# A retention, attention and token-mixing kernel: two-stage weight conversion, a later product of the values, other PSUM banks in the first and last batch, and attention outputs issued ahead of a state product

## The chip, the cores and the metric

The kernel runs on one core of a Trainium2 chip. Its engines work at the same time and wait for each other by semaphores: TensorE (PE in the profile; PEld is its weight load) for matrix products, VectorE (DVE), ScalarE (ACT), GpSimd (POOL), and SyncE (SP), whose queue issues nearly all DMA transfers. Each engine takes its instructions strictly in the order of its queue. The metric is the device time of one execution in microseconds (us); lower is better.

## The reference

```python
def _attn_ref(q, k, v):                      # 8 batches, 8 heads, 576 positions, 64 wide
    scores = scale * np.matmul(q, k.transpose(0, 1, 3, 2))
    gamma = 1.0 - 2.0 ** (-5.0 - np.arange(H, dtype=np.float32))
    Dmat = np.where(rel >= 0, gamma[:, None, None] ** rel[None, :, :], 0.0)
    return np.matmul(scores * Dmat[None], v)
def _moe_ref(x, w_gate, wq, wk, wv, wo):     # 4 experts, each position takes 2
    logits = x @ w_gate                      # the two best, softmax over them: the weights w
    for e in range(E):                       # causal softmax attention of every expert
        q = x @ wq[e]; k = x @ wk[e]; v = x @ wv[e]
        ye = softmax(causal(scale * (q @ k.T))) @ v @ wo[e]
        out += mask[..., None] * w[:, :, kk:kk + 1] * ye
def _moe2_ref(x, w_theta, w_tok_r, w_tok_i, w_ch):
    theta = x @ w_theta
    zr, zi = x * np.cos(theta), x * np.sin(theta)
    y = einsum('ts,bsd->btd', w_tok_r, zr) + einsum('ts,bsd->btd', w_tok_i, zi)
    u = x + y
    return u + np.maximum(u @ w_ch, 0.0)
```

The three run one behind the other: retention gives x, the experts' attention gives the next x, and the token mixing gives the result. Several weights come as float64.

## The kernel before

**First stage (0 to about 485 us).** Retention goes by chunks of 128 positions (five in a batch, the last of 64): `ret_scores` (`w<-kt`), `ret_values` (`w<-sm,vp`, then `w<-kt,S`) and `ret_state` (`pS<-vp,kv`), which adds to a state in the PSUM tile `pS`. After each half chunk ACT copies that state to SBUF (`S<-pS`), and the next `ret_state` may write `pS` only then. `ret_step` interleaves the three for one visit, in five visits a batch, which the table `SLOTS` calls R1 to R5. `loads` brings a chunk's keys and values (`kv`) and has POOL scale the values (`vp<-kv,gam`). The chunk's result is split into a rounded part `xh` (ACT) and a rest `xl` (POOL), from which `proj_qk` and `proj_v` project for the experts.

Between the visits the attention of the batch before runs by units of one expert pair and 128 rows: `at_scores`, `at_trans` (transposes through PSUM, copied to `PT` by DVE and ACT), and `at_out` (`w<-PT,V`), whose results ACT copies to `ob`. Also in this stage 52 blocks of float64 weights are converted: `convert` has five integer operations on DVE (`b`, `ex`), two on ACT (`r`, and `hl`, the rounded part) and three on POOL (`r`, `d`, `hl`), and the result is stored to DRAM.

PE stands in the order of the code in this stage. On the other engines, and on all of them later, a scheduler lays the queues out before the run by its own estimate of when each instruction is ready.

**Second stage (from about 485 us).** Eight batches, each with `mix(b, 0)`, some `token_tile`, `mix(b, 1)`, more `token_tile` and four `channel`. A `mix` sums 54 pairs of products, of 256 and 320 columns (`TS`), into four PSUM banks `acc`; DVE then adds them to `u`, ACT rounds them (`uh`), and DVE or POOL takes the rest (`ul`). `channel` puts its sums into banks called `w`. `z_tile` makes the operands of a mix from the angles `nr`: three operations on DVE, a sine on ACT, a product on DVE, then the split into `zh` and `zl`. `load_o` fetches the attention outputs of a batch and has POOL multiply them by the gate weights (`ol<-ol,og`). `x_put` and `x_get` transpose the next batch's input through DRAM.

Of the kernel before, what the change touches and what calls it, by code (L numbers as in the profile page):

```python
# [10 lines left out]
F32 = mybir.dt.float32  # L11
# [21 lines left out]
TS = [(0, 256), (256, 576)]  # L33
CV = 192
# [26 lines left out]
def tile_kernel(ctx: ExitStack, tc: tile.TileContext, qk, kv, w1, wo, wot, wd, cst, out):  # L61
# [20 lines left out]
    ident = consts.tile([128, 128], F32, name="ident")  # L82
    tri = att.tile([128, 64], F32, name="tri")
# [24 lines left out]
    QKT, KVT, XT, PSS, VP, SM, PX = {}, {}, {}, {}, {}, {}, {}  # L108

    def loads(b, c):  # L110
# [77 lines left out]
    def ret_step(b, c, nx):  # L188
# [234 lines left out]
    def convert(cvt, h, l, src, n):  # L423
# [30 lines left out]

    def cvt_jobs(pl, weights):

        def job(dst, off, o, n):
            t = pl.tile([128, 2, n], F32R, name="hl", bufs=2, padded_shape=[128, 2, CV])
            convert(pl, t[:, 0, :], t[:, 1, :], wd[:, off + o:off + o + n], n)
            flush()  # L460
            PEND.append((dst[:, :, o:o + n], t.bitcast(F32)))

        return [lambda a=(dst, off, x, min(CV, w - x)): job(*a) for dst, off, w in weights for x in range(0, w, CV)] + [flush]

# [412 lines left out]
```

## Time and profile before

| what | value |
|---|---|
| time, three runs | 912.73 us median (907.61 to 915.47) |
| profiled execution | 907.77 us, span 905.8 us, mean granted clock 0.992 |
| PE busy / PEld busy | 863.0 us (95%) / 803.9 us (89%) |
| DVE / ACT / POOL busy | 628.8 us (69%) / 454.9 us (50%) / 218.9 us (24%) |
| chain of waits, share by engine | PE 67%, DVE 10%, DMA 8%, ACT 6%, issue 3%, POOL 2%, SP queue 2% |

The span runs from the first to the last instruction. "Busy" of PE counts each product until its modelled end, so products that follow at once overlap. [...] An idle time is given with the instruction that it ends at and what released that one.

### The profile page before, as it was taken

The numbers are of one execution on the slowest core, as the hardware profiler recorded it, in microseconds if no ns is written. First come the engines' busy times: TensorE is split into PE (matmuls) and PEld (weight loads), VectorE is DVE, ScalarE is ACT, GpSimd is POOL, SyncE is SP. The second block draws the span as 40 slices with busy tenths as digits, with TensorE's granted clock in tenths as the row PEclk, the third lists the DMA queues.
The fourth block names the chain that finished last, engine by engine and source line by source line (L and its number), as shares of the span: only waits on it lengthen the run. The fifth ranks groups of instructions, "written<-read, shape, count | busy, mean of one in ns | idle before, by whom it ended". The sixth has DMA issues, their size and how long they took to land.

```text
span 905.8 us, 25503 instructions
## 1 busy us (share of the span) xinstructions
PE 863.0 (95%) x10062; PEld 803.9 (89%) x10062; DVE 628.8 (69%) x1779; ACT 454.9 (50%) x1198; POOL 218.9 (24%) x268
## 2 busy tenths in 40 slices
PE   6998999899999999998999989999999999999998
PEld 6987888788898888888878889999999999999998
DVE  5376767878787776777769947866578764676732
ACT  2466666666666665665656513443244533434320
POOL 2434152452535434242212102001020110001010
PEclk8999999999999999999999999999999999999999
DMA  7857566676667667656795152333425123251401
GB/s 276 237 143 234 159 203 170 187 223 184 194 182 241 167 180 227 163 148 207 202 317 173 30 143 50 62 90 92 128 50 135 35 72 80 37 125 25 106 23 53
DMA packets 146216, 130.30 MB, mean 144 GB/s; under 512 B 83504, under 2 KB 121648, under 8 KB 146096
## 3 DMA queue, kind: packets, MB, share of 16 engines
q1 hardware_dynamic: 145952, 128.39, 50.1%
q8 instruction: 79, 1.29, 0.6%
q0 software_dynamic: 144, 0.28, 0.2%
q14 instruction: 41, 0.34, 0.1%
HBM read 78.03 MB, written 32.00 MB: 121 GB/s over the span
## 4 chain that ended last, share of the span: by engine, by line
PE 67%; DVE 10%; DMA 8%; ACT 6%; issue 3%; POOL 2%; SPq 2%; DVEq 0%; ACTq 0%; POOLq 0%
PE acc L711 22%; PE w L99 9%; PE w L98 9%; PE w L100 9%; PE w L242 4%; PE w L370 4%; PE w L304 3%; DMA kv<-kv 3%; PE w L351 2%; ACT P L312 2%; PE pS L150 2%; DVE P L307 1%; DMA TK<-td 1%; DMA wst<-w 1%; ACT U L225 1%
## 5 line engine op out<-in xcount | busy, mean ns | idle before, releaser
L711 PE MATMUL acc<-TK,zh 128*128 128x256 f32 (+1 forms) x1024 | 180.7, 299 | 3.4 <-ACT zh L103 1.8
L711 PEld LDWEIGHTS acc<-TK,zh 128*128 128x128 f32 x1024 | 155.7, 191 | 4.0 <-issue 3.7
L312 ACT ACTIVATE P<-P,st 128x128 f32<-128x128 f32 (+4 forms) x160 | 95.6, 598 | 55.9 <-DVE st L307 55.5
L711 PE MATMUL acc<-TK,zl 128*128 128x256 f32 (+1 forms) x512 | 110.9, 298 | 0.0
L727 POOL TENSOR_TENSOR ul<-u,uh 128x576 fp32r<-128x576 f32 x16 | 24.3, 1540 | 336.4 <-ACT uh L726 336.4
L307 DVE CUSTOM_DVE_ANT_0 P<-w,cm 128x128 f32<-128x128 f32 (+4 forms) x160 | 71.8, 477 | 24.4 <-PE w L304 24.1
L711 PEld LDWEIGHTS acc<-TK,zl 128*128 128x128 f32 x512 | 87.0, 191 | 0.0
L103 ACT ACTIVATE zh<-cs 128x512 fp32r<-128x512 f32 x64 | 40.4, 631 | 90.2 <-PE acc L711 68.2
L99 PE MATMUL w<-xl,WH 128*128 128x288 f32 x256 | 75.9, 296 | 4.5 <-POOL xl L183 4.5
L567 ACT ACTIVATE cs<-cs 128x512 f32<-128x512 f32 x72 | 45.2, 631 | 69.1 <-DVE cs L565 55.2
L98 PE MATMUL w<-uh,CH 128*128 128x256 f32 (+1 forms) x256 | 75.5, 297 | 2.4 <-ACT uh L726 2.4
L98 PE MATMUL w<-xh,WH 128*128 128x288 f32 x256 | 76.0, 297 | 0.7 <-ACT PT L356 0.7
L104 DVE TENSOR_TENSOR zl<-cs,zh 128x512 fp32r<-128x512 f32 x64 | 44.0, 690 | 46.4 <-ACT zh L103 45.7
L304 PE MATMUL w<-KK,U 128*64 128x288 f32 (+4 forms) x384 | 76.2, 327 | 0.0
L99 PE MATMUL w<-ul,CH 128*128 128x256 f32 (+1 forms) x256 | 75.7, 296 | 0.0
L100 PE MATMUL w<-uh,CH 128*128 128x256 f32 (+1 forms) x256 | 75.6, 296 | 0.0
L100 PE MATMUL w<-xh,WL 128*128 128x288 f32 x256 | 75.4, 295 | 0.0
L150 PE MATMUL pS<-vp,kv 64*64 64x64 f32 x1024 | 44.0, 226 | 19.8 <-ACT S L153 15.9
L442 POOL TENSOR_TENSOR r<-r,ex 128x192 f32<-128x192 f32 (+1 forms) x51 | 29.5, 579 | 136.4 <-ACT hl L443 61.8
L569 DVE SCALAR_TENSOR_TENSOR cs<-cs,x 128x512 f32<-128x512 f32 x72 | 48.7, 687 | 18.6 <-ACT cs L567 18.4
L304 PEld LDWEIGHTS w<-KK,U 128*128 128x128 f32 (+1 forms) x384 | 53.9, 171 | 7.5 <-issue 4.3
L150 PEld LDWEIGHTS pS<-vp,kv 64*64 64x64 f32 x1024 | 35.8, 137 | 27.1 <-ACT S L153 18.5
(140 smaller groups left out, 2267.2 us busy)
## 6 DMA issues: line engine op xcount, KB each, us to landing
KK<-KN SPq DMA_DIRECT2D x128, 144.0 KB
kt<-qk SPq DMA_DIRECT2D x32, 512.0 KB
kv<-kv SPq DMA_DIRECT2D x32, 512.0 KB
raw<-wd SPq DMA_DIRECT2D x43, 192.0 KB
xd<-xb SPq DMA_DIRECT2D x126, 64.0 KB
out<-u SPq DMA_DIRECT2D x28, 288.0 KB
u<-xd SPq DMA_DIRECT2D x28, 288.0 KB
td<-hl SPq DMA_DIRECT2D x27, 192.0 KB
```

Source lines behind the costliest of these rows:

```text
L98: nc.tensor.matmul(ps, ah, bh, start=first, stop=False)
L99: nc.tensor.matmul(ps, ah, bl, start=False, stop=False)
L100: nc.tensor.matmul(ps, al, bh, start=False, stop=last)
L103: nc.scalar.activation(h, src, AF.Copy)
L104: nc.vector.tensor_sub(l, src, h)
L150: nc.tensor.matmul(pS[half(s), x, :], u[half(s), j, 0, x * D:x * D + D], vp[half(s), j, x, :], start=k == 0 and x == 0, stop=False, skip_g ...
L304: nc.tensor.matmul(ps[s][:R], U[:, s, rs], KK[:, s, x, j0:j1], start=x == 0, stop=x == 1)
L307: MARK["dve"] = nc.vector.tensor_tensor_reduce(Ps[s][:R, j0:j1], ps[s][:R], cm[:R, o + j0:o + j1], 1.0, st[:R, 0, s:s + 1] if i else 3.0e3 ...
L312: MARK["act"] = nc.scalar.activation(Ps[s][:R, :n], Ps[s][:R, :n], AF.Exp, bias=st[:R, last, s:s + 1], scale=-1.0, accum_out=SUM[p][:R, m, ...
L567: nc.scalar.activation(cs, cs, AF.Sin)
L569: nc.vector.scalar_tensor_tensor(z, cs, -1.0, x2[:, None, ds].to_broadcast([128, 2, 256]), op0=OP.mult, op1=OP.mult)
L711: nc.tensor.matmul(acc[d][j], A[:, dc], TK[:, kt, W, t0:t1], start=q == 0 and n == 0, stop=q == 8 and n == 2)
```

## The change

Seven edits:

1. `convert` ends after the first sums and returns `rest` (POOL's product and sums, ACT's `hl`), which the next block's job runs first. Its small tiles have two buffers, and the store goes out one job later.
2. `loads` no longer has the values scaled; `scale` does that at the end of a later visit.
3. `ret_step` takes `mid`, which issues the visit's `at_out`s ahead of the last state product.
4. The gate product of `load_o` waits for the channel products issued last (from batch 1 on).
5. In `z_tile`, DVE's subtraction of half pi becomes a bias of ACT's sine, which is split into two.
6. `mix` (from batch 1 on) and `channel` use equal halves of 288 columns (`TH`).
7. In batches 0 and 7, `mix(b, 1)` sums into the banks `w` and `channel` into the banks `acc`. In batch 0 `x_put` stands among the channels.

```diff
+TH = [(0, 288), (288, 576)]
...
-        vp = ret.tile([128, 2, 4, D], F32, name="vp", bufs=VPB)
-        MARK["pool"] = nc.gpsimd.tensor_mul(vp[:, :n], u[:, :n, 1, :].rearrange("p j (h d) -> p j h d", h=4),
-                                            gam[:, c, :n, :, None].to_broadcast([128, n, 4, D]))
-        QKT[b, c], KVT[b, c], VP[b, c] = t, u, vp
+        QKT[b, c], KVT[b, c] = t, u
+        RAW.append((b, c))
+
+    def scale_v(b, c):
+        n = ROWS[c] // 64
+        vp = VP[b, c] = ret.tile([128, 2, 4, D], F32, name="vp", bufs=VPB)
+        MARK["pool"] = nc.gpsimd.tensor_mul(vp[:, :n], KVT[b, c][:, :n, 1, :].rearrange("p j (h d) -> p j h d", h=4),
+                             gam[:, c, :n, :, None].to_broadcast([128, n, 4, D]))
+
+    def scale():
+        if RAW:
+            scale_v(*RAW.pop(0))
...
-            if nx[1] < NCH - 1:
-                diag.append(ret_state(nx[0], 2 * nx[1]))
         if c >= 0:
             off.append(ret_values(b, c))
-        for _ in zip_longest(chain(*diag), chain(*off)):
+        last = nx and nx[1] < NCH - 1
+        off = chain(*off)
+        for _, _ in zip_longest(chain(*diag), islice(off, 12) if last and mid else off):
             pass
+        if mid:
+            mid()
+        for _ in zip_longest(ret_state(nx[0], 2 * nx[1]) if last else (), off):
+            pass
+        if (b, c) > (0, 1):
+            scale()
...
-        nc.gpsimd.tensor_mul(r, r, ex.bitcast(F32))
-        nc.scalar.activation(h, v, AF.Copy)
-        d = tmp("d", F32)
-        nc.gpsimd.tensor_sub(d, v, h)
-        nc.gpsimd.tensor_add(l, d, r)
...
+        def rest():
+            nc.gpsimd.tensor_mul(r, r, ex.bitcast(F32))
+            nc.scalar.activation(h(), v, AF.Copy)
+            nc.gpsimd.tensor_sub(v, v, h())
+            nc.gpsimd.tensor_add(l(), v, r)
+
+        return rest
...
+    def finish():
+        flush()
+        if REST:
+            rest, pl, n, dst = REST.pop()
+            t = pl.tile([128, 2, n], F32R, name="hl", bufs=2, padded_shape=[128, 2, CV])
+            HL[:] = [t]
+            rest()
+            PEND.append((dst, t.bitcast(F32)))
...
-        nc.gpsimd.tensor_mul(OL[b], OL[b], gw)
+        m = nc.gpsimd.tensor_mul(OL[b], OL[b], gw)
+        if "ch" in MARK:
+            tc.add_manual_dep(m.ins, MARK["ch"].ins.name, mybir.DependencyInfo(
+                mybir.DependencyClass.Sync, mybir.DependencyReason.DATA), reason="behind the channel products")
...
-        nc.vector.tensor_scalar(cs[:, 0, :], cs[:, 0, :], math.pi / 2.0, None, op0=OP.subtract)
         nc.vector.tensor_scalar(cs[:, 1, :], nr[:, ds], PI_LO, -PI_LO, op0=OP.min, op1=OP.max)
-        nc.scalar.activation(cs, cs, AF.Sin)
+        nc.scalar.activation(cs[:, 0, :], cs[:, 0, :], AF.Sin, bias=quarter)
+        nc.scalar.activation(cs[:, 1, :], cs[:, 1, :], AF.Sin)
...
-                ret_step(x, c - 1, (x, c) if c < NCH else (x + 1, 0) if x + 1 < B else None)
-                for o in outs:
-                    at_out(*o)
-                outs = []
+                def mid():
+                    for o in outs:
+                        at_out(*o)
+                    outs.clear()
+
+                ret_step(x, c - 1, (x, c) if c < NCH else (x + 1, 0) if x + 1 < B else None, mid)
...
-        acc = [[ps2.tile([128, t1 - t0], F32, name=f"acc{d}{i}", bufs=1, padded_shape=[128, 512])
-                for i, (t0, t1) in enumerate(TS)] for d in range(2)]
+        ts = TH if b else TS
+        spare = h and b in EDGE
+        acc = [[ps2.tile([128, t1 - t0], F32, name="w" if spare else f"acc{d}{i}", bufs=4 if spare else 1,
+                         padded_shape=[128, 512]) for i, (t0, t1) in enumerate(ts)] for d in range(2)]
...
+    EDGE = (0, B - 1)
...
-        for t0, t1 in TS:
-            ps = ps2.tile([128, t1 - t0], F32, name="w", bufs=4, padded_shape=[128, 512])
+        for j, (t0, t1) in enumerate(TH):
+            spare = b in EDGE
+            ps = ps2.tile([128, t1 - t0], F32, name=f"acc{et % 2}{j}" if spare else "w", bufs=1 if spare else 4,
+                          padded_shape=[128, 512])
...
         for et in range(4):
             channel(b, et)
+            for x in q[2 * et:2 * et + 2] if not b else []:
+                x_put(*x)
+        if not b:
+            x_get(1)
```

The visit R1, on PE. `w<-PT,V` are the attention outputs, `pS<-vp,kv` the visit's last state product, `w<-kt,S` the last products of the values. Before:

```order
L134 MATMUL w<-kt 64x64 x2
L170 MATMUL w<-kt,S_134 64x64 x2
L150 MATMUL pS<-vp,kv 64x64 x8
L370 MATMUL w<-PT,V 64x128 x2
L370 MATMUL w<-PT,V 64x256 x4
L370 MATMUL w<-PT,V 64x128 x2
L304 MATMUL w<-KK,U 64x288 x8
```

And now:

```order
L145 MATMUL w<-kt 64x64 x2
L181 MATMUL w<-kt,S_136 64x64 x2
L387 MATMUL w<-PT,V 64x128 x2
L387 MATMUL w<-PT,V 64x256 x4
L387 MATMUL w<-PT,V 64x128 x2
L161 MATMUL pS<-vp,kv 64x64 x8
L321 MATMUL w<-KK,U 64x288 x8
```

The outputs have moved ahead of the state product; R3 and R5 change in the same way, while R2 has no outputs and R4 no last state product.

The visit R3, on ACT, between the exponentials of a unit and `xh`. `r` and `hl` belong to a conversion. Before:

```order
L312 ACTIVATE P,sum_127<-P,st 128x128 x2
L441 ACTIVATE r<-raw 128x192
L443 ACTIVATE hl<-b_2392 128x192
L245 COPY V<-w 128x256
L246 ACTIVATE lg_124<-w 128x4
L356 COPY PT<-w 128x4x64
L358 COPY PT<-w 64x64
L153 ACTIVATE S_135<-pS 128x256
L153 ACTIVATE S_136<-pS 128x256
```

And now:

```order
L329 ACTIVATE P,sum_129<-P,st 128x128 x2
L465 ACTIVATE hl<-b_2228 128x128
L461 ACTIVATE r<-raw 128x192
L262 COPY V<-w 128x256
L263 ACTIVATE lg_126<-w 128x4
L373 COPY PT<-w 128x4x64
L375 COPY PT<-w 64x64
L164 ACTIVATE S_137<-pS 128x256
L391 COPY ob<-w 128x192
L164 ACTIVATE S_138<-pS 128x256
```

`hl` now belongs to the block before (its size differs from that of `r`), and the copy of an attention output stands between the two state copies.

POOL, two visits of one batch, with the buffers' numbers, which count up in the order of the code (`kv_2069` is loaded at the end of the visit whose result is `xt_2063`). Before:

```order
L119 TENSOR_TENSOR vp_2071<-kv_2069,gam_121 128x512
L183 TENSOR_TENSOR xl_2062<-xt_2063,xh_2061 128x4x128
L442 TENSOR_TENSOR r_2244<-r_2244,ex_2240 128x128
L445 TENSOR_TENSOR d_2248<-b1_2237,hl_2234 128x128
L446 TENSOR_TENSOR hl_2234<-d_2248,r_2244 128x128
L119 TENSOR_TENSOR vp_2232<-kv_2230,gam_121 128x256
L183 TENSOR_TENSOR xl_2062<-xt_2224,xh_2061 128x4x128
```

And now:

```order
L127 TENSOR_TENSOR vp_2218<-kv_2086,gam_123 128x512
L194 TENSOR_TENSOR xl_2079<-xt_2080,xh_2078 128x4x128
L466 TENSOR_TENSOR b1_1960<-b1_1960,hl_2221 128x192
L464 TENSOR_TENSOR r_2235<-r_2235,ex_2231 128x128
L467 TENSOR_TENSOR hl_2221<-b1_1960,r_1967 128x192
L127 TENSOR_TENSOR vp_2372<-kv_2216,gam_123 128x256
L194 TENSOR_TENSOR xl_2079<-xt_2210,xh_2078 128x4x128
```

The product of the values just loaded (`kv_2086` with `xt_2080`) still stands directly ahead of that visit's `xl`; only the operations of the conversions have moved.

POOL, at the end of the first stage. `ol<-ol,og` are gate products, `ul<-u,uh` belongs to the first mixes. Before:

```order
L446 TENSOR_TENSOR hl<-d,r 128x128
L520 TENSOR_TENSOR ol<-ol,og 128x1152 x2
L727 TENSOR_TENSOR ul<-u,uh 128x576 x4
L520 TENSOR_TENSOR ol<-ol,og 128x1152
L727 TENSOR_TENSOR ul<-u,uh 128x576 x2
```

And now:

```order
L467 TENSOR_TENSOR hl<-b_8315,r 128x128
L770 TENSOR_TENSOR ul<-u,uh 128x576 x2
L556 TENSOR_TENSOR ol<-ol,og 128x1152
L770 TENSOR_TENSOR ul<-u,uh 128x576 x2
L556 TENSOR_TENSOR ol<-ol,og 128x1152
L770 TENSOR_TENSOR ul<-u,uh 128x576 x2
```

The two gate products of batches 2 and 3 have left the end of the first stage and stand behind the `ul` of batch 0 and of batch 1.

## Rows read from the trace of the kernel before

**Rows 1.** Windows: us; then busy us (instructions) by engine, granted clock, DMA.
```profile
150.00:200.00 50.00, 46.23 (x842) 41.63 (x840) 40.03 (x130) 32.89 (x103) 22.74 (x31) 1.00 0.69 198
700.00:750.00 50.00, 50.00 (x344) 48.08 (x343) 35.16 (x81) 20.80 (x37) 5.77 (x3) 1.00 0.30 77
```

**Rows 2.** Waits of PE, 50 to 410 us: total us, times, longest.
```profile
PE pS L150 <- ACT S L153: 12.8, 17, 2.1
PE w L99 <- POOL xl L183: 4.5, 5, 1.9
PE w L242 <- POOL xl L183: 1.7, 1, 1.7
```

**Rows 3.** Waits of PE, 410 to 906 us.
```profile
PE w L98 <- ACT uh L726: 2.4, 1, 2.4
PE acc L711 <- ACT zh L103: 1.8, 1, 1.8
PE acc L711 <- DVE u L725: 1.6, 1, 1.6
...
PE acc L711 <- DVE u L723: 1.5, 1, 1.5
```

**Rows 4.** Timeline of PE, a visit R1: start, duration, instructions, idle before.
```profile
164.93 0.23 PE L170 MATMUL w<-kt,S 64*64 64x64 f32 x2
165.72 0.68 PE L150 MATMUL pS<-vp,kv 64*64 64x64 f32 x16 [0.56 <-ACT S L153]
166.33 1.52 PE L370 MATMUL w<-PT,V 128*64 128x128 f32 x16
```

**Rows 5.** Timeline of ACT, the same visit.
```profile
165.11 0.27 ACT L358 COPY PT<-w 128x128 f32<-128x128 f32 x1
165.26 0.40 ACT L153 ACTIVATE S<-pS 128x256 f32<-128x256 f32 x1
```

**Rows 6.** Timeline of all engines, a visit R3.
```profile
176.06 1.43 DVE L434 SCALAR_TENSOR_TENSOR b<-raw,b 128x192 int32<-128x192 int32 x1
...
177.92 0.36 ACT L443 ACTIVATE hl<-b 128x192 fp32r<-128x192 f32 x1 [1.26 <-DVE b L438]
...
178.43 0.20 DVE L358 COPY PT<-w 64x64 f32<-64x64 f32 x1
...
178.86 0.39 ACT L153 ACTIVATE S<-pS 128x256 f32<-128x256 f32 x1
...
179.30 0.27 PE L150 MATMUL pS<-vp,kv 64*64 64x64 f32 x2 [2.12 <-ACT S L153]
```

**Rows 7.** Timeline of POOL, a visit R5.
```profile
143.23 1.04 POOL L119 TENSOR_TENSOR vp<-kv,gam 128x512 f32<-128x512 f32 x1 [3.11 <-DMA kv<-kv]
144.23 0.72 POOL L183 TENSOR_TENSOR xl<-xt,xh 128x256 fp32r<-128x256 f32 x1
```

**Rows 8.** Timelines of POOL, DVE, ACT and PE, 475 to 489 us.
```profile
475.01 2.68 POOL L520 TENSOR_TENSOR ol<-ol,og 128x1152 f32<-128x1152 f32 x1 [17.46 <-DMA og<-gd]
...
475.60 2.24 DVE L564 TENSOR_SCALAR cs<-nr 128x256 int32<-128x256 int32 x1
...
483.59 0.31 ACT L374 COPY ob<-w 128x192 f32<-128x192 f32 x1
...
483.88 0.68 DVE L552 TENSOR_TENSOR nr<-k,pS 128x512 f32<-128x512 f32 x1
...
484.76 1.20 PE L711 MATMUL acc<-TK,zh 128*128 128x256 f32 x4 [1.79 <-ACT zh L103]
```

**Rows 9.** Windows, the stretch behind that, columns as in the first group.
```profile
484.90:488.30 3.40, 3.40 (x15) 3.38 (x16) 3.10 (x10) 2.40 (x4) 0.00 (x0) 0.50 0.74 188
```

**Rows 10.** Timeline of DVE, before the channels of batch 0.
```profile
521.72 1.54 DVE L725 COPY u<-acc 128x256 f32<-128x256 f32 x4
```

**Rows 11.** Timeline of PE: six products of a mix; then fifteen of 288 columns.
```profile
599.76 0.43 PE L711 MATMUL acc<-TK,zl 128*128 128x256 f32 x2
...
600.56 0.43 PE L711 MATMUL acc<-TK,zl 128*128 128x256 f32 x2
...
150.10 0.30 PE L98 MATMUL w<-xh,WH 128*128 128x288 f32 x1
...
152.09 0.29 PE L98 MATMUL w<-xh,WH 128*128 128x288 f32 x1
```

**Rows 12.** Groups of instructions by line: count, busy us, mean ns.
```profile
L564 DVE TENSOR_SCALAR cs<-nr 128x256 int32<-128x256 int32 x72 | 25.6, 356 | 0.8
...
L565 DVE TENSOR_SCALAR cs<-cs 128x256 f32<-128x256 f32 x72 | 20.4, 283 | 0.0
```

More of the change, by code (lines that the diff above doesn't have):

```diff
@@ L3 @@
 from contextlib import ExitStack
-from itertools import chain, zip_longest
+from itertools import chain, islice, zip_longest
 import concourse.bass as bass
@@ L82, in tile_kernel @@
     ident = consts.tile([128, 128], F32, name="ident")
+    quarter = consts.tile([128, 1], F32, name="quarter")
+    nc.vector.memset(quarter, -math.pi / 2.0)
     tri = att.tile([128, 64], F32, name="tri")
@@ L107, in tile_kernel @@
     MARK = {}
-    QKT, KVT, XT, PSS, VP, SM, PX = {}, {}, {}, {}, {}, {}, {}
+    QKT, KVT, XT, PSS, VP, SM, RAW = {}, {}, {}, {}, {}, {}, []
     def loads(b, c):
@@ L186, in ret_values, with ret_step @@
             loads(*nx)
-    def ret_step(b, c, nx):
+    def ret_step(b, c, nx, mid=None):
         diag, off = [], []
@@ L393, in tile_kernel @@
     loads(0, 0)
+    scale_v(0, 0)
     nc.sync.dma_start(tri, cst[:, 256:320])
     loads(0, 1)
+    scale_v(0, 1)
     o += NCH * H
@@ L416, in tile_kernel @@
         loads(0, c)
+        scale_v(0, c)
     with tc.issue_after(MARK["pool"].ins):
@@ L427, in convert, with tmp @@
         lo, hi = raw[:, :, 0], raw[:, :, 1]
-        def tmp(name, dt):
-            return cvt.tile([128, n], dt, name=name, bufs=1, padded_shape=[128, CV])
+        def tmp(name, dt, bufs=2):
+            return cvt.tile([128, n], dt, name=name, bufs=bufs, padded_shape=[128, CV])
         b1 = tmp("b1", I32)
@@ L441, in convert @@
         nc.scalar.activation(r, lo.bitcast(U32), AF.Copy, scale=2.0 ** -52)
-        nc.gpsimd.tensor_mul(r, r, ex.bitcast(F32))
-        nc.scalar.activation(h, v, AF.Copy)
-        d = tmp("d", F32)
-        nc.gpsimd.tensor_sub(d, v, h)
-        nc.gpsimd.tensor_add(l, d, r)
-    PEND = []
+        def rest():
[4 more added lines that the diff above has]
+        return rest
+    PEND, REST = [], []
     def flush():
@@ L453, in flush @@
             nc.sync.dma_start(dst, t)
+    def finish():
[6 more added lines that the diff above has]
+            PEND.append((dst, t.bitcast(F32)))
+    HL = []
     def cvt_jobs(pl, weights):
         def job(dst, off, o, n):
[L458 to L463, printed above, removed]
+            finish()
+            rest = convert(pl, lambda: HL[0][:, 0, :], lambda: HL[0][:, 1, :], wd[:, off + o:off + o + n], n)
+            REST.append((rest, pl, n, dst[:, :, o:o + n]))
+        return [lambda a=(dst, off, x, min(CV, w - x)): job(*a) for dst, off, w in weights
+                for x in range(0, w, CV)] + [finish, flush]
     FW = []
@@ L500, in tile_kernel @@
         make_gt(c)
+    RAW[:3] = []
+    scale()
     w1s.release()
@@ L709, in mix @@
                 for n, (A, W) in enumerate(((zh, 0), (zh, 1), (zl, 0))):
-                    for j, (t0, t1) in enumerate(TS):
+                    for j, (t0, t1) in enumerate(ts):
                         nc.tensor.matmul(acc[d][j], A[:, dc], TK[:, kt, W, t0:t1], start=q == 0 and n == 0,
@@ L720, in mix @@
             k = 2 * h + d
-            for j, (t0, t1) in enumerate(TS):
+            for j, (t0, t1) in enumerate(ts):
                 if b:
@@ L739, in channel @@
             o = u[:, et, t0:t1]
-            nc.vector.scalar_tensor_tensor(o, ps, 0.0, o, op0=OP.max, op1=OP.add)
+            MARK["ch"] = nc.vector.scalar_tensor_tensor(o, ps, 0.0, o, op0=OP.max, op1=OP.add)
             if b == B - 1:
@@ L783, in tile_kernel @@
                 token_tile(ps2, *x)
-            x_put(*x)
+            if b:
+                x_put(*x)
         mix(b, 1)
@@ L788, in tile_kernel @@
                 token_tile(ps2, *x)
-            x_put(*x)
-        if b + 1 < B:
+            if b:
+                x_put(*x)
+        if 0 < b < B - 1:
             x_get(b + 1)
@@ L793, in tile_kernel @@
             channel(b, et)
+            for x in q[2 * et:2 * et + 2] if not b else []:
+                x_put(*x)
+        if not b:
+            x_get(1)
     ps2.release()
```

## The prediction

> **What bounds the kernel now.** I read the windows first, then PE's waits, then the timelines around the longest of them. In the second stage a window of 50 us holds 50.00 us of busy PE, while DVE stands at 35.16 and ACT at 20.80 [rows 1]. There the columns streamed by PE are the time, and nothing done on the other engines can show. In the first stage PE is busy 46.23 us of 50 [rows 1]; the few us missing in each window are all that can be won. They have names. Between 50 and 410 us PE waits 12.8 us, in 17 waits, for ACT's copy of the state before it may write `pS` again, and 6.2 us for `xl` of POOL [rows 2]. Around and after the change of stage it waits 1.8, 1.6, 2.4 and 1.5 us [rows 3]. So there are some 26 us to win in 900, and each edit is costed by the gap of PE that it closes. The sum is made against the profiled execution (907.77 us) and carried over to the median of the runs, 912.73 us, 5.0 us higher.
>
> **The change part by part.**
>
> *Outputs ahead of the state product, R1.* PE issues its last `w<-kt,S` at 164.93; pairs of these follow each other at .06 us, so the state product could start at 164.99. It starts at 165.72, .73 us later, when ACT's state copy (165.26 + .40) is done; behind it come the outputs, which take 1.45 us to the next row (166.33 to 167.78, of which the row shows 1.52 busy) [rows 4, 5]. Now the outputs run from 164.99, end near 166.4, and find the copy done. They need `PT` themselves: ACT's last copy of it ends at 165.38 [rows 5], before the output that reads it, which is the last of 16. Seven of the 17 waits of [rows 2] are R1's, alike within .06 us: 7 x .73 = 5.1 us; bounds 3.9 (7 x .56, the idle as the row counts it) to 5.5. R2 has seven more and no outputs to move, so it keeps them; R5 never waited. What moves with the outputs: ACT's `ob` copies come ahead of the second state copy, which only the next visit reads, and in R3 the values' last products, and with them `xt`, `xh` and `xl`, come some 1.7 us later, a unit or more before a projection reads them.
>
> *R3.* Three of the 17 waits stand there, 2.12 us in the row (2.3, 1.8 and .6 start to start). The row above tells why the state copy is late: ACT stood 1.26 us at `hl` of a conversion, which waited for a DVE operation of 1.43 us, and only then reached its `PT` copies and the state copy at 178.86 [rows 6]. Edit 1 puts `hl` of the block before in that place, so ACT runs on. But the outputs now stand first, and they need DVE's `PT` copy, which ended at 178.63 behind the same slow operation [rows 6]: .6 to .7 us before PE's start at 179.30. I take 2.0 us for the three, the nearer end being this row; bounds 0.5 and 4.7 (all of it, if the slow operation is gone too).
>
> *The later product of the values* is worth nothing. The order shows POOL's product of the chunk just loaded in the place it had, directly ahead of that visit's `xl`; in R5 that pair is the wait of 3.11 us for the DMA and the `xl` behind it, at which PE stands afterwards [rows 7]. The 6.2 us [rows 2] stay. Since the conversions' operations and stores move on POOL and SP, the loads may land earlier or later: 0, bounds 3 us won and 2 lost. What else edit 1 moves (ACT's and POOL's share of a block one job later, the store two) is queued in engines with 17 and 27 us of slack per 50 [rows 1]: nothing.
>
> *The gate products, and the sines at the change of stage.* POOL's product of batch 2 runs from 475.01 for 2.68 us, and the DVE operation that opens the first `z_tile` lasts 2.24 us, to 477.84, instead of the mean of .356 [rows 8, 12]. DVE reaches its last reading of the old `pS` bank at 483.88 + .68 = 484.56, and PE starts its first mix at 484.76, after 1.79 us of idling [rows 8]. Then the clock is at 0.50 for 3.4 us [rows 9]: fifteen products where 3.4 us hold some 25 at .133, which costs about 1.4 us. The order takes that gate product out of this place (and ACT's two splits that hang on it from ahead of `ob`). DVE is then 1.9 us earlier and what ends last is the copy of `ob`, done at 483.90 in the row and earlier without the splits. With the .2 us that PE took behind DVE's reading, PE starts between 483.4 and 484.1; I take 483.5, since the `PT` outputs that `ob` copies end near 483.0. That is 1.2 us, plus 1.4 us of the clock if it no longer falls: 2.6; bounds 0.6 (start at 484.1, clock falls again) and 3.8. At its new place the product also holds `og`, which has one buffer, so SP's transfer of the next `og` waits; the order puts that transfer behind `x_get`, a visit before it is read.
>
> [...]
>
> *The banks of batches 0 and 7.* `mix(b, 1)` no longer waits until DVE has emptied the banks of `mix(b, 0)`: 1.6 and 1.5 us of idling [rows 3], 1.79 and 1.68 start to start; 3.4 us, bounds 2.5 and 3.5. The channels of batch 0 wait 2.4 us for `uh`, because DVE's copies of `u` start at 521.72 [rows 10], 1.7 us after the mix has ended, behind sine operands and a transpose. In the new order that transpose stands ahead of the two operand products, and .283 us of DVE is gone from each `z_tile` [rows 12]; but four of the five transposes still stand ahead of the copies. I take 1.1 us, bounds 0 and 1.7. In exchange the first products of `mix(1, 0)` need the banks of the last channels; the last bank is used .9 us into the mix, and DVE empties it in some .45 us: nothing, bound .5 us lost. `x_put` and `x_get` of batch 1 come later on DVE and SP, by most of the channels; their data is read where `mix(1, 0)` ends, 14 us on (54 pairs at .267).
>
> *Equal halves.* Three pairs of 256 and 320 columns take .80 us (599.76 to 600.56), .267 a pair; fifteen products of 288 take 1.99 us (150.10 to 152.09), .1327 each, .265 a pair [rows 11]. There are 756 pairs in the mixes of batches 1 to 7 and 384 in the channels: 1140 x .0019 = 2.1 us, bounds 0 and 3.4 (medians of .118 + .149 and 2 x .132).
>
> [...]
>
> *Sines.* 72 subtractions of .283 us leave DVE [rows 12], and ACT's 72 sines become 144 of half the length. Both have cover in the second stage (14.8 and 29.2 us idle per 50, [rows 1]): nothing, beyond what is counted above.
>
> Sum: 5.1 + 2.0 + 0 + 2.6 + 3.4 + 1.1 + 2.1 = **16.3 us**. That is 891.5 us against the profiled execution, and 896.4 against the median.
>
> **The rivals.**
>
> *The outputs wait for their own operands.* They now come .6 to 2.3 us nearer to the copies of `PT`. If DVE's or ACT's copy is what ends last (conversions stand between a unit's row minima and its `PT` copies), R1 gives .2 us a visit, R3 nothing, and R5, which had no wait, gets one of .2: the sum falls by 5.1 + 2.0 and gains and loses 1.4: 9.2, 903.5. Against it: the margin of the last `PT` copy in R1 [rows 5]. For it: R3 [rows 6].
>
> *The second-stage edits do not do what they say.* [...] Had something else set the start of the first mix (the `ob` copy, the transfers of TK), and did the mixes of the edge batches wait for `zh` instead of banks, 2.6 + 3.4 + 1.1 would shrink to about 1: sum 10.2, 902.5.
>
> *The gate products block DVE at their new places.* All six come at the opening of a visit or right behind its first mix. If each does there what the row at 475 shows (1.8 us of PE idle and 1.4 of clock, 3.2 us), the price is 19.2 us, against 13.7 from the other parts: 918, slower. It decides where DVE's work in that stretch is what PE waits for next. Against it: the window of 700 to 750 us holds such a product among POOL's 5.77 us, and PE idles not at all [rows 1].
>
> *More than forecast*: R3 whole (2.7 more) and half of `xl` (3.1): sum 22.1, 891.
>
> **How the numbers follow.** A change of 1% (9.1 us) is about what a measurement of this kernel can tell from none. Chances: forecast 0.62, outputs waiting .16, second stage .12, gate products .04, more .06. Without `xl` the low ends add to 7.0 us and the high ends to 22.6, with its gain to 25.6; on the median that is 887 to 906. All parts hardly lie at one end together, so I take 888 to 905, which leaves out about 0.15. Faster by over 1% (under 903.6): .62 + .06 + half of the two rivals near that line, .14 = .82. Slower by over 1%: .03. The rest, .15, is within.
>
> **What would show it.** In the changed profile: no wait of `pS` for ACT in R1, seven of some .6 us left in R2, R3's at `PT` or gone; `xl` waits still there; no idle above .6 us and no 0.50 ahead of the first mix; no wait of `acc` for `u`; pairs in the mixes at .265 us. I am wrong if PE's waits moved to `PT` in sum, or if busy PE in the second stage falls below 50.00 per 50 us beside a gate product.

## The result, and the profile after

The changed kernel is .7% slower: 917.17 us median of 13 runs (914.0 to 922.76) against 910.45 us of the kernel before (13 runs); ratio 1.0068, 95% interval 1.0048 to 1.0088. The forecast was 896.4. The profiled execution took 917.17 us (span 915.1, mean granted clock 0.986 where it was 0.992).

The windows of the changed kernel, to be held against [rows 1], with two short ones behind long waits:

```profile
150.00:200.00 50.00, 44.51 (x825) 39.22 (x823) 39.53 (x121) 30.76 (x99) 20.86 (x28) 1.00 0.69 202
300.00:350.00 50.00, 44.02 (x688) 39.26 (x688) 35.47 (x122) 28.32 (x89) 17.25 (x25) 0.97 0.64 183
700.00:750.00 50.00, 50.00 (x344) 48.08 (x344) 33.48 (x73) 22.82 (x46) 3.08 (x2) 1.00 0.34 80
200.60:204.00 3.40, 3.40 (x15) 3.39 (x16) 0.14 (x1) 0.41 (x1) 1.54 (x3) 0.52 0.01 1
533.00:537.00 4.00, 4.00 (x17) 4.00 (x18) 2.33 (x5) 1.41 (x3) 0.00 (x0) 0.50 0.00 0
```

The second stage is as full as it was. The first stage has lost PE time (44.51 against 46.23 in one window), and in places PE now works at a granted clock of 0.50. The waits of PE, from 50 to 410 us (against [rows 2]) and behind 410 us (against [rows 3]), show which:

```profile
PE w L102 <- POOL xl L194: 12.0, 5, 3.0
PE pS L161 <- ACT S L164: 6.8, 9, 1.3
PE w L387 <- DVE PT L373: 5.7, 6, 1.7
PE w L368 <- DVE sm L149: 1.6, 2, 0.8
...
PE acc L101 <- ACT uh L769: 3.4, 1, 3.4
...
PE acc L754 <- ACT ob L391: 0.5, 1, 0.5
```

The wait for the state copy has gone from 12.8 to 6.8 us: those of R1 are gone and R2's are left, as forecast, but in two batches R2 waits longer than the .6 us forecast (1.3 us). But `xl` has doubled, from 6.2 to 12.0, `PT` and `sm` are new, and the channels' wait for `uh` has grown from 2.4 to 3.4. To see when the time was lost, the table takes the start of the same work on PE in both profiled executions:

| work on PE | before | after | after minus before |
|---|---|---|---|
| R5 of the fourth batch, first scores | 193.89 | 191.85 | -2.0 |
| the unit's scores behind it | 203.88 | 205.86 | +2.0 |
| same place, fifth batch | 257.92 | 264.19 | +6.3 |
| same place, sixth batch | 311.49 | 322.41 | +10.9 |
| a last unit of the first stage | 424.76 | 438.93 | +14.2 |
| first product of the first mix | 484.76 | 496.77 | +12.0 |
| first channel product, batch 0 | 519.7 | 528.3 | +8.6 |
| first channel product, batch 1 | 577.6 | 589.3 | +11.7 |
| first channel product, batch 6 | 845.7 | 856.9 | +11.2 |
| end of the span | 905.8 | 915.1 | +9.3 |

Three steps of that difference, of 3.6 to 4.4 us, stand at R5 of three batches; two of 3.2 us stand between R1 and R2 of two batches (shown at e8). One of the three, in the timelines of PE, POOL and SP's queue of the changed kernel:

```profile
191.85 0.27 PE L145 MATMUL w<-kt 64*64 64x64 f32 x2
...
197.32 0.30 PE L101 MATMUL w<-xh,WH 128*128 128x288 f32 x1
200.54 0.44 PE L102 MATMUL w<-xl,WH 128*128 128x288 f32 x1 [2.92 <-POOL xl L194]
```

```profile
186.36 0.60 POOL L466 TENSOR_TENSOR b<-b,hl 128x192 f32<-128x192 f32 x1 [0.57 <-ACT hl L465]
187.61 0.59 POOL L464 TENSOR_TENSOR r<-r,ex 128x192 f32<-128x192 f32 x1 [0.65 <-DVE ex L459]
188.16 0.59 POOL L467 TENSOR_TENSOR hl<-b,r 128x192 fp32r<-128x192 f32 x1
...
198.76 1.04 POOL L127 TENSOR_TENSOR vp<-kv,gam 128x512 f32<-128x512 f32 x1 [7.63 <-DMA kv<-kv]
199.76 0.72 POOL L194 TENSOR_TENSOR xl<-xt,xh 128x256 fp32r<-128x256 f32 x1
```

```profile
188.78 0.53 SPq L476 DMA_DIRECT2D td<-hl  x1
189.40 2.62 SPq L237 DMA_DIRECT2D KK<-KN  x4
192.12 0.55 SPq L117 DMA_DIRECT2D kt<-qk  x1
192.71 0.44 SPq L120 DMA_DIRECT2D kv<-kv  x1
```

Read from the end: PE stands 2.92 us for `xl`, behind which it runs at 0.52 (the window from 200.6). `xl` stands on POOL behind `vp` of the chunk just loaded, and that waits for the transfer of `kv`. The transfer was issued .86 us after R5's first product. Ahead of it in SP's queue stand `KK` and the conversion's store `td`, which goes out as soon as POOL's sum `hl` is done (188.16 + .59 = 188.75). And that sum stands behind POOL's product `r,ex`, which waited for DVE: this is the product of the next block, which the scheduler has put between the two sums of the block before. The order printed ahead of the prediction shows it (`r_2235` between `b1_1960` and `hl_2221`). So far this is read from one execution; the experiments try it.

### The profile page after: what moved, and what is told of

It is laid out like the page before. It is cut to its first block, busy times and chain, and to the rows that moved or that the text cites. A ratio compares the mean times of both kernels' runs of the same rounds, so it can differ in the third digit from the quotient of the medians.

```text
span 915.1 us, 25431 instructions
## 1 busy us (share of the span) xinstructions
PE 868.8 (95%) x10062; PEld 808.2 (88%) x10062; DVE 626.3 (68%) x1708; ACT 463.0 (51%) x1270; POOL 221.1 (24%) x268
## 4 chain that ended last, share of the span: by engine, by line
PE 74%; DVE 9%; DMA 6%; issue 5%; POOL 2%; ACT 2%; SPq 1%; DVEq 0%; ACTq 0%; POOLq 0%
PE acc L754 22%; PE w L102 9%; PE w L103 9%; PE w L101 9%; PE w L259 4%; PE w L321 4%; PE w L387 4%; DMA kv<-kv 3%; PE w L368 3%; PE pS L161 2%; PE w L754 2%; PE w L145 1%; DVE b L458 1%; PE w L181 1%; PE acc L101 1%
## 5 line engine op out<-in xcount | busy, mean ns | idle before, releaser
L754 PE MATMUL acc<-TK,zh 128*128 128x288 f32 (+2 forms) x896 | 155.9, 296 | 0.5 <-ACT ob L391 0.5
L754 PEld LDWEIGHTS acc<-TK,zh 128*128 128x128 f32 x896 | 131.9, 189 | 0.8 <-issue 0.6
L754 PE MATMUL acc<-TK,zl 128*128 128x288 f32 (+1 forms) x448 | 95.8, 295 | 0.0
L102 PE MATMUL w<-xl,WH 128*128 128x288 f32 x256 | 77.7, 304 | 12.1 <-POOL xl L194 12.0
L324 DVE CUSTOM_DVE_ANT_0 P<-w,cm 128x128 f32<-128x128 f32 (+4 forms) x160 | 71.9, 476 | 12.0 <-PE w L321 11.7
L754 PEld LDWEIGHTS acc<-TK,zl 128*128 128x128 f32 x448 | 72.3, 189 | 0.0
L605 ACT ACTIVATE cs<-cs,quarter 128x256 f32<-128x256 f32 x72 | 36.5, 506 | 60.0 <-DVE cs L603 58.0
L387 PE MATMUL w<-PT,V 128*64 128x192 f32 (+3 forms) x576 | 55.4, 324 | 8.0 <-DVE PT L373 8.0
L102 PEld LDWEIGHTS w<-xl,WH 128*128 128x128 f32 x256 | 49.6, 194 | 14.1 <-POOL xl L194 13.4
L127 POOL TENSOR_TENSOR vp<-kv,gam 128x512 f32<-128x512 f32 (+1 forms) x40 | 38.7, 967 | 96.4 <-DMA kv<-kv 66.0
L368 PE MATMUL w<-ident,P 128*128 128x128 f32 (+2 forms) x480 | 59.4, 258 | 1.8 <-DVE sm L149 1.6
L466 POOL TENSOR_TENSOR b<-b,hl 128x192 f32<-128x192 f32 (+1 forms) x51 | 30.9, 605 | 122.8 <-ACT hl L465 121.5
```

What stands on the lines that cost most here:

```text
L102: nc.tensor.matmul(ps, ah, bl, start=False, stop=False)
L324: MARK["dve"] = nc.vector.tensor_tensor_reduce(Ps[s][:R, j0:j1], ps[s][:R], cm[:R, o + j0:o + j1], 1.0, st[:R, 0, s:s + 1] if i else 3.0e3 ...
L368: nc.tensor.transpose(tp[:w, j, :], Ps[s][:R, j * C:j * C + w], ident[:R, :R])
L387: nc.tensor.matmul(po[s * 64:s * 64 + 64, c0:], V[:ROWS[j], j, 2 * p + s, :], v, start=j == 0, stop=j == last, skip_group_check=True)
L754: nc.tensor.matmul(acc[d][j], A[:, dc], TK[:, kt, W, t0:t1], start=q == 0 and n == 0, stop=q == 8 and n == 2)
```

## The experiments

The ratios are to the kernel before, run on the same chip.

**Edit 3 alone** (`e1_mid_only`):

```diff
-                ret_step(x, c - 1, (x, c) if c < NCH else (x + 1, 0) if x + 1 < B else None)
-                for o in outs:
-                    at_out(*o)
+                ret_step(x, c - 1, (x, c) if c < NCH else (x + 1, 0) if x + 1 < B else None, mid)
```

> The kernel before with edit 3 alone (outputs ahead of the state product). Theory 1, the won time is waited away at xl: R1 steps gain .63 us seven times (4.4), but PE reaches each R5 earlier while the load of kv lands when it did, so waits of w for xl of POOL grow from 6.2 by 2 to 4 us; 0 to 2 us faster than before, more if the clock does not fall, slower by up to 3 if it falls to 0.50 behind the longer waits. Theory 2, the conversions do the harm and the outputs are innocent: 4 to 6 us faster, xl waits within 1.5 us of 6.2.

Measured .9946 (.9924 to .9968), 4.9 us faster, as theory 2 has it. Its waits, 50 to 410 us:

```profile
PE pS L150 <- ACT S L153: 4.9, 8, 0.7
PE w L99 <- POOL xl L183: 3.9, 4, 1.9
PE w L374 <- DVE PT L360: 3.4, 2, 1.7
PE w L246 <- POOL xl L183: 2.4, 3, 1.3
```

`xl` stays at 6.3 us: where PE comes earlier, `kv` comes earlier with it (at R5 of the fourth batch it is issued .40 us ahead of the first scores product, before .26). Of the forecast rival there is a piece, 3.4 us of `PT` in two visits R3.

**The changed kernel without edit 3** (`e2_no_mid`):

```diff
-        if mid:
-            mid()
-        for _ in zip_longest(ret_state(nx[0], 2 * nx[1]) if last else (), off):
+            if nx[1] < NCH - 1:
+                diag.append(ret_state(nx[0], 2 * nx[1]))
```

> The changed kernel without edit 3 (outputs behind the state product again). Theory 1: the seven R1 waits of .6 to .7 us for the state copy come back (4.4 us), the xl waits shrink by about as much and the half clock behind them goes at one to three places (1.6 us each): 0 to 5 us faster than the changed kernel, 912 to 917 against 917.2. Theory 2 (conversions): the waits for PT (8.0 us) and sm (1.6) go to the state copy instead; within 2 us of the changed kernel.

Measured 1.0104 (1.0069 to 1.014), 3 us slower than the changed kernel's 1.0068, if anything; theory 1's gain did not come, and `xl` still waits 12.1 us. The outputs' new place does no harm.

**Edit 1 alone** (`e3_convert_only`):

```diff
-        nc.gpsimd.tensor_mul(r, r, ex.bitcast(F32))
-        nc.scalar.activation(h, v, AF.Copy)
...
+        def rest():
+            nc.gpsimd.tensor_mul(r, r, ex.bitcast(F32))
+            nc.scalar.activation(h(), v, AF.Copy)
```

> The kernel before with edit 1 alone (two-stage conversion, two buffers). Theory 1: little harm by itself, R3's 2.1 us of waits for the state copy go, some come back elsewhere; within 2 us of the kernel before. Theory 2: DVE's conversion operations now stand ahead of sm, xt and the copies of PT and wait there for the raw transfer, which costs 3 us at each of two places and 1.4 at three: 5 to 10 us slower than before.

Measured 1.0177 (1.0141 to 1.0214), 16 us slower, more than either theory said. Its longest waits from 50 to 410 us:

```profile
PE pS L150 <- ACT S L153: 13.6, 17, 1.4
PE w L99 <- POOL xl L183: 13.1, 5, 3.2
```

The 13.1 us at `xl` are the 12.0 of the changed kernel again, with no other edit present: edit 1 brings them. How it does so was not in my theory 2. The state copy's waits, which edit 1 was counted on to shorten in R3, are still 17.

**The values' product behind `xl`** (`e4_xl_first`), the changed kernel with one order edge:

```diff
+        MARK["xl"] = nc.gpsimd.tensor_sub(xl[:, :, cs], xt, xh[:, :, cs])
...
+            with tc.issue_after(MARK["xl"].ins):
+                scale_v(*RAW.pop(0))
```

> The changed kernel, with POOL's product of the values put behind xl of the visit in which it is issued, by an order edge; nothing else differs. Theory 1: the 12.0 us of waits of w for xl go, and with them the stretches at 0.50 behind three of them (1.6 us each): 12 to 17 us faster than the changed kernel, 900 to 905; some of it can come back as waits of the state product for vp. Theory 2: what holds the first stage is the conversions on DVE, xl would be late anyway behind xt: under 5 us faster, 912 or more.

Measured .9858 (.9819 to .9896): 2.1% below the changed kernel, 19 us, and so theory 1, above its upper end. No wait for `xl` is left in its first lines:

```profile
PE pS L162 <- ACT S L165: 4.9, 7, 1.0
PE w L388 <- DVE PT L374: 4.6, 11, 1.2
PE w L369 <- DVE sm L150: 1.6, 2, 0.8
```

**Edit 2 alone** (`e5_values_only`):

```diff
-        MARK["pool"] = nc.gpsimd.tensor_mul(vp[:, :n], u[:, :n, 1, :].rearrange("p j (h d) -> p j h d", h=4),
...
+        RAW.append((b, c))
...
+        if (b, c) > (0, 1):
+            scale()
```

> The kernel before with edit 2 alone (values scaled by a later call). The order on POOL keeps the product of the chunk just loaded directly ahead of that visit's xl, so nothing changes: within .3% of the kernel before, xl waits 5 to 7 us. If the later call matters by itself, the xl waits differ by over 3 us in sum.

Measured .9988 (.9967 to 1.0009): nothing, as forecast; `xl` waits 7.3 us. The later call by itself doesn't move the product.

**The changed kernel without edit 1** (`e6_no_convert`):

```diff
-        def rest():
-            nc.gpsimd.tensor_mul(r, r, ex.bitcast(F32))
...
+        nc.gpsimd.tensor_mul(r, r, ex.bitcast(F32))
+        nc.scalar.activation(h, v, AF.Copy)
```

> The changed kernel without edit 1 (conversion in one stage, single buffers). If edit 1 is what made the changed kernel slow, the first stage is as with edit 3 alone (4 us ahead of before where the units begin to end, near 455 us of before) and the second gains 4 to 5 us as in the changed kernel: ratio to before .990 (.986 to .994). If edits 2 and 1 do the harm together, or the second stage costs time by itself, over .996.

Measured .9857 (.982 to .9895), 13.0 us below the kernel before, a little more than forecast. So with the other six edits present edit 1 costs 2.1%, or 19 us. This kernel still waits for `xl`, as the kernel before did (4.5 and 2.7 us):

```profile
PE w L387 <- DVE PT L373: 4.9, 4, 1.7
PE pS L161 <- ACT S L164: 4.9, 8, 0.7
PE w L102 <- POOL xl L194: 4.5, 4, 2.1
PE w L259 <- POOL xl L194: 2.7, 2, 1.4
```

The profiled executions of the two, held against each other by the same work on PE, are 14.9 us apart at the end of the attention units: 12.4 us arise at the three R5s (3.7, 4.5 and 4.2), 6.3 between R1 and R2 of two batches, and the other places give back 3.8.

**Edits 4 to 7 alone** (`e7_stage2_only`), the kernel before with

```diff
+            tc.add_manual_dep(m.ins, MARK["ch"].ins.name, mybir.DependencyInfo(
...
+        nc.scalar.activation(cs[:, 0, :], cs[:, 0, :], AF.Sin, bias=quarter)
...
+        ts = TH if b else TS
+        spare = h and b in EDGE
```

> The kernel before with edits 4 to 7 alone. The forecast was 9.2 us for them; the trace of the changed kernel shows 4.9 us between the last units and the end, with a wait of 3.4 us for uh and a stretch at 0.50 behind it. First stage unchanged. If those two belong to the second-stage edits, 4 to 5 us faster (ratio .995); if they came from the shifted first stage, 8 to 9 us (.990).

Measured .995 (.9918 to .9983), 4.5 us, half of the forecast 9.2; its wait for `uh` is 3.6 us, so that wait belongs to these edits and not to a shifted first stage.

**Without edit 1, and the values' product behind `xl`** (`e8_no_convert_xl`), e6 with

```diff
+            with tc.issue_after(MARK["xl"].ins):
+                scale_v(*RAW.pop(0))
```

> The changed kernel without edit 1 and with POOL's product of the values behind the visit's xl. Theory 1: relative to the run without edit 1 it saves that run's xl waits (6 to 7 us) and more where the clock fell behind them: ratio to before .982 to .985, 1 to 3 us ahead of the changed kernel with that product moved (.986), since the waits of DVE's conversions for sm and PT (4 to 5 us there) go as well. If, with xl out of the way, edit 1 is worth something by its own purpose (ACT running on in R3), the two are level or the changed kernel with the product moved is ahead.

Measured .980 (.9767 to .9833), a little below e4 (.9858); the intervals overlap. Of the steps by which PE in e4 falls behind e8, the largest are two of 2.8 and 3.2 us between R1 and R2. There `sm` is late, because DVE stands at a conversion whose `raw` transfer has not landed. In the changed kernel one of them is, on DVE and then PE:

```profile
165.79 0.26 DVE L453 TENSOR_SCALAR b<-raw 128x192 int32<-128x192 int32 x1 [2.21 <-DMA raw<-wd]
...
166.91 0.69 DVE L149 TENSOR_TENSOR sm<-w,tri 128x512 f32<-128x512 f32 x1
```

```profile
167.66 1.25 PE L368 MATMUL w<-ident,P 128*128 128x128 f32 x8 [0.82 <-DVE sm L149]
```

The next two ask what in edit 1 makes `kv` late.

**The next block's product behind the sum** (`e9_mul_last`), the changed kernel with one order edge:

```diff
-            nc.gpsimd.tensor_mul(r, r, ex.bitcast(F32))
+            with ExitStack() as es:
+                if "l" in MARK:
+                    es.enter_context(tc.issue_after(MARK["l"].ins))
+                nc.gpsimd.tensor_mul(r, r, ex.bitcast(F32))
...
+            MARK["l"] = nc.gpsimd.tensor_add(l(), v, r)
```

> The changed kernel with one order edge on POOL: the next block's product r,ex stands behind the sum hl of the block before, instead of between that block's two sums. Theory: that product waits for DVE's ex, and behind it wait hl, the store td at the head of SP's queue, the four KK transfers, kt and kv; where R5 begins, kv was issued .5 to .9 us after R5's first product instead of .3 to 1.2 ahead of it. With the edge hl and td come about 1.2 us earlier and kv .6 to 1.2, so each of the three long xl waits shrinks by about that and some of the half clock goes: 3 to 8 us faster than the changed kernel (ratio to before .998 to 1.004). Rival: KN is late by DVE's conversion operations alone, and kv stays where it is: within 2 us of the changed kernel.

Measured .9986 (.9959 to 1.0014), 7.5 us below the changed kernel, at the upper end of the theory. (The profiled execution took 903.23 us, the median is 907.65.) The chain at R5 of the fourth batch, each worked out from the timelines as us from R5's first scores product:

| | kernel before | changed | e9 | e6, no edit 1 |
|---|---|---|---|---|
| DVE's rest of `KN` done | -5.08 | -3.69 | -4.50 | -5.09 |
| POOL's `hl` done | -5.00 | -3.10 | -4.22 | -5.06 |
| `td` issued | -4.97 | -3.08 | -4.20 | -5.04 |
| first `KK` issued | -4.36 | -2.45 | -3.57 | -4.43 |
| `kv` issued | -0.26 | +0.86 | -0.25 | -0.20 |
| POOL's `vp` begins (`kv` has landed) | +4.42 | +6.91 | +4.54 | +4.80 |

PE is ready for `xl` at about +5.6 in the changed kernel, and `vp` and `xl` take 1.7 us on POOL. So `kv` 2.5 us later against R5 makes the difference between a short wait and one of 2.92 us. About 1.1 us of it is the later issue; the rest is a longer way from issue to landing (6.05 us against 4.68), whose cause was not tried apart. In the changed kernel the next `kt` follows `kv` at once in the queue (193.25).

The other two R5s are less clean:

| | kernel before | changed | e9 | e6, no edit 1 |
|---|---|---|---|---|
| fifth batch, `kv` issued | -1.00 | +0.52 | +0.45 | -0.77 |
| fifth batch, `vp` begins | +3.82 | +7.00 | +5.39 | +3.96 |
| sixth batch, `kv` issued | -1.21 | +0.77 | +0.01 | -1.16 |
| sixth batch, `vp` begins | +3.96 | +6.99 | +5.53 | +3.99 |

At the fifth batch the edge hardly moves the issue. In e9 POOL's sum waits for ACT's `hl` (1.15 us at 185.88, the fourth batch), and at the fifth DVE ends the rest of `KN` only 3.83 us ahead of R5's first product (5.09 in e6), behind five operations of a conversion. So the rival has a share: the hoisted product is one part of what makes `kv` late, and edit 1's places on DVE and ACT are the likely rest.

**One buffer for the conversion** (`e10_one_buf`), the changed kernel:

```diff
-        def tmp(name, dt, bufs=2):
+        def tmp(name, dt, bufs=1):
```

> The changed kernel with one buffer instead of two for b1, ex and r. The product r,ex can't be hoisted then, and DVE's operations of a block wait for the sum hl of the block before. If the hoisted product is the harm: as the run with the order edge, 3 to 8 us faster than the changed kernel. If DVE's place of the conversion ahead of KN, sm and PT is the harm: no better, or slower, since DVE now waits for POOL inside its queue.

Measured 1.0302 (1.0274 to 1.033), the slowest of all. With one buffer DVE's first operation of each block, and ACT's `r`, wait inside their queues for POOL's sum of the block before, ahead of `PT` and `sm`, which PE needs. The longest waits of DVE and ACT (50 to 410 us), and a row of PE's over the whole execution:

```profile
DVE b L453 <- POOL hl L467: 40.0, 40, 2.7
```

```profile
ACT r L461 <- POOL hl L467: 41.9, 37, 1.8
```

```profile
PE w L387 <- ACT PT L373: 9.8, 12, 2.0
```

So in two stages the second buffer is worth its place, and with it the scheduler is free to hoist. This run doesn't tell the hoisted product's price, since it adds a wait of its own.

**Both edges** (`e11_xl_mul`), e9 with

```diff
+            with tc.issue_after(MARK["xl"].ins):
+                scale_v(*RAW.pop(0))
```

> The changed kernel with both order edges on POOL: values' product behind xl, r,ex behind the sum of the block before. With xl out of the way the late kv no longer holds PE, so the second edge should be worth little: .983 to .986 (the first edge alone: .986). If the two-stage conversion's remaining harm (.986 against .980 without edit 1) is the hoisted product, .980; if it is the place on DVE (waits for sm 1.6 and PT 6.1 us), it stays at .985.

Measured .9849 (.9828 to .987), level with e4. With `xl` out of the way a late `kv` holds nobody. What edit 1 still costs, .5% against e8 (.980), stands between R1 and R2 of the same two batches: PE loses 3.0 and 2.6 us there against e8, where `sm` is late on DVE.

**The copies of `u` first** (`e12_best_u`), e8 with DVE's operands for batch 1's first mix behind the copies of batch 0's second:

```diff
+                    MARK["u"] = nc.vector.tensor_copy(u[:, k, t0:t1], acc[d][j])
...
+                    if b == 1:
+                        es.enter_context(tc.issue_after(MARK["u"].ins))
+                    z_tile(g, i, h)
```

> The kernel without edit 1 and with the values' product behind xl, and DVE's operands of batch 1's first mix put behind the copies of u of batch 0's second mix. In the run without this edge PE waits 3.4 us for uh ahead of the channels of batch 0 and runs some 3.4 us at 0.50 behind it (1.6 us lost). Theory: the wait falls to about 1 us (PE's last product, two copies .8, uh .7, less the eight products in front) and the clock does not fall: 3.5 to 4.5 us faster, ratio to before .975 to .977. Rival: the first mix of batch 1 then waits for its operands and gives it back: .980.

Measured .9748 (.9721 to .9774): 885.35 us, 4.7 us below e8 and the fastest of all. The wait for `uh` is gone altogether, and so is the half clock behind it: its windows there show PE without a gap. The rival, that the first mix of batch 1 then waits, did not come.

```profile
500.00:505.00 5.00, 5.00 (x37) 4.64 (x36) 3.21 (x8) 1.88 (x3) 0.00 (x0) 1.00 0.41 65
505.00:510.00 5.00, 5.00 (x40) 5.00 (x40) 4.86 (x13) 2.37 (x5) 0.00 (x0) 1.00 0.24 72
```

## Why the prediction was wrong

**The step that failed** is the one sentence on what else edit 1 moves: "queued in engines with 17 and 27 us of slack per 50 [rows 1]: nothing". Edit 1 measured 16 us lost alone (e3) and 19 us in the changed kernel (e6 against it), and the loss against the kernel before is gone without it. Slack of an engine says how much work it can still take; it doesn't say that the operation which someone waits for is not behind one that itself waits. About 14 of the 19 us need `xl` behind `vp`, since with that order turned edit 1 costs some 5 (e11 and e4 against e8, whose intervals just overlap). Edit 1 lets a product that waits for DVE stand ahead of POOL's `hl`; `hl` is what `td` waits for, `td` stands ahead of `KK`, `kt` and `kv` in SP's queue, `kv` is what `vp` waits for, and `vp` stands ahead of `xl`. The edge of e9 on that product won 7.5 us. The other 6 or 7 of the 14 were not tried apart; the table of the fifth and sixth batch points at the places of the conversion on DVE and ACT and at a longer way to landing. The 5 us that do not need `xl` stand on DVE: at two visits `sm` is late behind a conversion that waits for `raw` (the rows at e8), with steps of 3.2 us at each. I had named the last two links and SP's store, and put both order rows before the reader, but read them as "only the operations of the conversions have moved", and did not ask who waits for those operations.

**The later product of the values** was right as to the edit (e5: nothing) and wrong as to its bounds. "The 6.2 us stay; bounds 3 us won and 2 lost" was 5.8 us lost in waits, and the bound had no term for the clock: behind the three waits of about 3 us PE works for some 3.4 us at 0.50 (windows of .52, .53 and .58 from 200.6, 258.9 and 317.3), which costs 1.3 to 1.5 us each (at the first, a step of 3.86 us less 2.33 of longer wait). 5.8 + 4.2 = 10.0 us. The edge of e4 won more than that, 19 us: it also removes the 6.2 us that the kernel before waited, and the waits for the state copy and `PT` are 1.9 and 1.1 us less there.

**Outputs ahead of the state product, R1**: right in mechanism and nearly in size, 7 x .63 = 4.4 us for 5.1. The rows that answer to [rows 4]:

```profile
162.89 1.52 PE L387 MATMUL w<-PT,V 128*64 128x128 f32 x16
164.34 0.68 PE L161 MATMUL pS<-vp,kv 64*64 64x64 f32 x16
164.95 1.01 PE L321 MATMUL w<-KK,U 128*64 128x288 f32 x6
```

The .1 us short of the forecast is in the first of them: the outputs begin .1 us behind the last `w<-kt,S`.

**R3**: forecast 2.0 us won, measured .8 lost (the steps of the six visits, -2.4, -.5, -.5, +1.6, +1.2 and +1.4). Where PE waited longest for the state copy it no longer does, but in three other visits `PT` is late by 1.4 to 1.7, which is the first rival. One of them, on DVE and then PE:

```profile
119.36 1.32 DVE L458 SCALAR_TENSOR_TENSOR b<-ex,b 128x192 f32<-128x192 int32 x1
120.71 0.40 DVE L459 TENSOR_SCALAR ex<-b 128x192 int32<-128x192 int32 x1
121.03 0.41 DVE L373 COPY PT<-w 128x256 f32<-128x256 f32 x1
```

```profile
121.50 1.73 PE L387 MATMUL w<-PT,V 128*64 128x192 f32 x18 [1.54 <-DVE PT L373]
```

One operation of a conversion is slow as in [rows 6] (there `b<-raw,b`): 1.32 us, where the median of its 51 is .36. POOL's `xl` runs beside it (119.04 + 1.42 = 120.46, this one ends .22 us later, at 120.68), and beside the slow one of [rows 6], which ends .21 us behind it (177.49 against 177.28); before, on POOL:

```profile
175.99 1.29 POOL L183 TENSOR_TENSOR xl<-xt,xh 128x512 fp32r<-128x512 f32 x1
```

That `xl` is what slows them was not tried in a run.

**The first mix**: forecast 2.6 us, measured 2.8. It begins .49 us behind the last output instead of 1.79, and released by the copy of `ob`, as forecast; the lag falls from 13.3 (the last work of the first stage) to 12.0 there, and to 10.5 four us on, since the clock no longer falls (PE's timeline, and the window behind it):

```profile
496.77 0.88 PE L754 MATMUL acc<-TK,zh 128*128 128x256 f32 x5 [0.49 <-ACT ob L391]
```

```profile
496.80:500.20 3.40, 3.40 (x26) 3.40 (x27) 2.90 (x7) 1.34 (x3) 0.00 (x0) 1.00 0.39 110
```

DVE's operation that opens the first `z_tile`, 2.24 us beside POOL's product in [rows 8], takes .28 there (at 488.89), with no POOL operation between 469.37 and 513.94. The rival of the gate products did not come: PE is busy 50.00 us of 50 in each of the windows that hold the six (540 to 590, 650 to 700 and 750 to 800).

**Banks**: forecast 3.4, measured 3.8 (10.5 to 8.6 at batch 0, 11.2 to 9.3 at batch 7). **Channels of batch 0**: forecast 1.1 won, measured 3.1 lost (8.6 to 11.7). I took DVE's chain ahead of the copies as shortened by the edits, and did not subtract that the banks let the mix end 2 us earlier against that chain. So the wait grew to 3.4 us, and behind it the clock fell (0.50 in the window from 533). DVE at that place:

```profile
530.72 0.68 DVE L107 TENSOR_TENSOR zl<-cs,zh 128x512 fp32r<-128x512 f32 x1
531.33 1.54 DVE L768 COPY u<-w 128x256 f32<-128x256 f32 x4
```

The copies stand behind operands of the next batch, and DVE idles less than a us in all between 515 and 533; e12 shows that the order was the cause.

**Equal halves**: forecast 2.1, measured .5 over five of the batches (11.7 to 11.2). Six products of 288 columns in a mix take what six of 256 and 320 did in [rows 11], .80 us:

```profile
611.38 0.43 PE L754 MATMUL acc<-TK,zl 128*128 128x288 f32 x2
...
612.19 0.42 PE L754 MATMUL acc<-TK,zl 128*128 128x288 f32 x2
```

(612.19 - 611.38 = .81.) The .1327 that I took came from a projection of the first stage. By the rows of the mixes themselves a pair takes .27 us either way, a gain of nothing, and the .5 us measured is nearer to that than to the 2.1.

Together: without edit 1 the forecast's terms sum to 14.3 us (16.3 less the 2.0 of R3), and e6 measured 13.0. That they come so near is in part luck: the second stage alone gave half of its 9.2 us (e7), with edit 3 (e1) 9.4 together. Where e6 makes up the other 3.6 was not taken apart; its profiled execution is only 6.6 us below that of the kernel before (901.20 against 907.77).

## What to carry to other kernels

Slack of an engine does not cover a change of order on it: for each moved instruction look at what it waits for, and who waits for the one now behind it, through every queue (here POOL, SP's queue, POOL again) until PE. A call made later in the code is not an instruction placed later when a scheduler lays the queues out; where the place matters, state it with an order edge: two of them, with edit 1 left out, turned a loss of .7% into a gain of 2.5%. And a gain upstream is spent at the next chain that does not move with it, as the banks' gain was at the copies of `u`.

## What was not expected of the hardware

After waits of PE of 2.9 to 3.4 us the clock was at 0.50 for some 3.4 us (windows of .52, .53, .58 and .50 at 200.6, 258.9, 317.3 and 532.9 in the changed kernel). After waits of 1.9 to 2.4 us it was at 1.00 (windows of 3.5 us from 145.0, 179.3 and 523.3 in the kernel before), but after the 1.79 us ahead of the first mix it was at 0.50 [rows 8, 9], with 15 products in 3.4 us where the window from 496.80 holds 26 at 1.00. So the length of the last wait did not decide it alone. At R5 the three waits cost 1.3 to 1.5 us each beyond their own length.

Kernels with `xl` behind the load's product vary by 5 to 11 us over ten runs or more, and by 3 to 5 over four; in e9 the mean clock goes with it (903.23 us at 0.991, 911.72 at 0.985), in e5 it doesn't (905.47 us at 0.992, 910.8 at 0.994); the four with the edge vary by 1 to 3 us over four (e4: 895.55 to 896.52). That the spread comes from these waits is only argued from this.
